# Normalising attention's output before a SwiGLU block: 32x32 transpositions on VectorE and one product in place of four sums and four transposes on TensorE

## The chip, the core and the metric

The kernel runs on one core of one Trainium2 chip. A time is the device time of one execution in microseconds (us). It stands here as the median of several runs; the profile is of one execution, in which every instruction on each engine has a start and a duration. [...] Each engine runs its own queue in order and waits on semaphores of the others.

## What is computed

Attention with normalised queries and keys, followed by a feed-forward block with a normalisation ahead of it (all f32, 8 sequences of 448 rows, 12 heads of 64, model width 768, inner width 1536):

```python
q_n, k_n = rmsnorm(q, g_q), rmsnorm(k, g_k)          # over the 64 of a head
scores = matmul(q_n, k_n.T) / sqrt(64)
attn = exp(scores - max); attn = attn / (sum(attn) + 1e-9)
x = (attn @ v) laid out as (8 * 448, 768)

rms = sqrt(mean(x * x, axis=-1) + 1e-6)
xn = x / rms * rms_g
g = xn @ w_gate
out = (g * sigmoid(g) * (xn @ w_val)) @ w_out
```

The change is in how `rms` of x is formed and spread.

## The kernel before

The kernel works on pairs of heads, six to a sequence, 48 in all, in one loop whose index is g = 6 b + hp. Attention's output for a pair comes out transposed: x of sequence b is a tile of 128 partitions (features of the pair) by 448 columns (rows of the sequence), six such tiles to a sequence. The sum of squares over the 768 features is therefore a sum over partitions and over the six tiles. ScalarE squares each pair's x, GpSimd adds it to the tile `ss` (128 x 448, L644), so that after the sixth pair each column of `ss` still has to be summed over 128 partitions.

Two functions finish it:

- `rms_x(b)` (L721 to L730): four products with a column of ones, one for each 112 columns of `ss`, which put the 448 sums into PSUM as 112 partitions x 4 columns (`msx`, L726); VectorE scales them and adds 1e-6 (L728), GpSimd raises to the power -0.5 (L730).
- `norm_x(b)` (L732 on): four transposes on TensorE of those columns, broadcast to 128 (L738), which give `rb`, the 448 factors on all partitions, in PSUM; six VectorE instructions multiply x by the gain and by `rb` (L744), spread over the next steps for b > 0. It then queues the sums of x blocks that the fast products read.

Sequence b of the feed-forward runs while attention of sequence b+1 goes on. Its products are done by a scheme with fewer multiplications, so that VectorE makes sums of blocks of x, of the weights and of the results (L1209, L1212, L1378, L1406 and others). Weight sums are made once, in sequences 1 to 3: `derive` (L1091, L1094), `derive_o` (L1126) and `derive_q` (L1154 to L1157) write them, SyncE stores them to DRAM (`kept`, `kept_o`, `kept_q`) and loads them back for the products. Before that, while sequence 0 is under way, the weights themselves are taken in and converted in three steps on VectorE (L917 to L919), two on ScalarE (L911, L912) and one on GpSimd (L968).

The order of all this is written out by hand. The main loop calls `pe(fn)` for each piece of TensorE work, `fill(n)` puts n pieces of feed-forward products between pieces of attention, and `after(n, fn)` has a piece of another engine's work issued n TensorE pieces later. No scheduler moves anything, so what is issued first on an engine runs first there. At the first pair of a sequence (hp == 0, b of 2 and more) the loop turns the next pair's queries and keys (`turn`, L545 and L549, transposes on TensorE), issues `rms_x(b - 1)` between the two turns, finishes the feed-forward products in hand (L1604 in sequence 0, L1191 after) with `fill(len(todo))`, and then issues `norm_x(b - 1)`. For sequence 0 the two functions are called one pair later, with their own lines. `invert` (L597 to L599) is in use for attention's sums: it transposes 32x32 blocks on VectorE, inverts 14 columns, and transposes them back with a broadcast.

PSUM holds four banks for scores (tag `s`, from which `msx` and `rb` are taken), one for attention's values and three for feed-forward products.

## Time and profile before

| | |
|---|---|
| three runs, us | 1515.65, 1513.07, 1515.41 |
| median, us | 1515.41 |
| span of the profiled execution, us | 1514.0 |
| granted TensorE clock, mean over the span | 0.997 |
| instructions in the span | 25709 |
| TensorE weight loads | 8732 |
| DMA | 322.51 MB, mean 213 GB/s |

The profiled execution is known by its span, from its first to its last instruction; the runs also hold what lies around that. The page gives each engine's busy time and the chain of work that ended last; further views give, for one line or tile, the durations of its instructions, for one engine what it waited for and what ended the wait, and for a stretch of time each instruction with its start. "PE" is TensorE's products, "PEld" its weight loads, "SPq" the issue of DMAs. A product of f32 tiles is recorded as two passes, a transpose as one.

### The profile page before, as it was taken

To read this page: it belongs to the slowest core of one execution; us is meant where nothing else is said; L and a number is where in the kernel's file an instruction comes from. 1 tells how busy PE (TensorE), PEld (TensorE's weight loads), DVE (VectorE), ACT (ScalarE), POOL (GpSimd) and SP (SyncE) were. 2 spreads that over 40 slices of the span, in tenths; PEclk is the share of its full clock that TensorE was granted. 3 is DMA by queue.
4 is the path that set the end of the run, shared out by engine and by line. 5 is a ranking of instruction groups with operands and counts; after the bars stand their busy time and mean duration, and the time that the engine had idled before them with its cause. 6 is when DMAs were issued, how large, how long until landed. Compare 5 with 4: busy or idle time off the path is not lost.

```text
span 1514.0 us, 25709 instructions
## 1 busy us (share of the span) xinstructions
PE 1478.8 (98%) x8732; PEld 1154.0 (76%) x8732; DVE 1037.7 (69%) x1826; ACT 602.2 (40%) x1377; POOL 741.3 (49%) x708
## 2 busy tenths in 40 slices
PE   8999999999899999999999999999999999999997
PEld 4344445678755888878888888768888789899997
DVE  5788999699944697874568555535668655684664
ACT  6856764344323433234343443443542433101100
POOL 6867997556423454564535643445645731021002
PEclk9999999999999999999999999999999999999999
DMA  7758675776667899996558855585558655587675
GB/s 200 227 159 252 174 247 174 228 249 206 224 219 224 266 316 312 301 291 180 163 150 257 244 176 153 165 255 159 153 153 255 216 162 139 165 292 234 174 228 180
DMA packets 302176, 322.51 MB, mean 213 GB/s; under 512 B 81620, under 2 KB 243668, under 8 KB 302036
## 3 DMA queue, kind: packets, MB, share of 16 engines
q1 hardware_dynamic: 301108, 320.58, 69.4%
q8 instruction: 72, 1.18, 0.3%
q14 instruction: 68, 0.56, 0.1%
q10 hardware_dynamic: 800, 0.20, 0.1%
q0 software_dynamic: 128, 0.00, 0.0%
HBM read 266.90 MB, written 53.77 MB: 212 GB/s over the span
## 4 chain that ended last, share of the span: by engine, by line
PE 84%; DVE 8%; DMA 3%; issue 1%; SPq 1%; POOL 1%; ACT 0%; DVEq 0%; POOLq 0%
PE ff L1191 37%; PE ff L1532 13%; PE sc L659 7%; PE av L674 7%; PE ff L1604 6%; PE ff L1461 5%; PE tr L545 2%; PE den L692 1%; PE den L607 1%; PE sc L563 1%; PE av L590 1%; PE ff L1334 1%; DVE l L1406 1%; DMA w<-kept 1%; DVE w L1091 1%
## 5 line engine op out<-in xcount | busy, mean ns | idle before, releaser
L1191 PE MATMUL ff<-x,w 128*128 128x224 f32 x1296 | 259.6, 353 | 1.4 <-DVE pb L1212 1.1
L714 POOL TENSOR_TENSOR es<-es,e 128x448 f32<-128x448 f32 x205 | 253.4, 1236 | 13.6
L1191 PEld LDWEIGHTS ff<-x,w 128*128 128x128 f32 x1296 | 242.7, 190 | 5.4 <-DVE pb L1212 1.4
L659 PE MATMUL sc<-qT,kT 64*64 64x448 f32 x1176 | 231.0, 539 | 0.7 <-DVE x L744 0.7
L674 PE MATMUL av<-e,vt 64*64 64x448 f32 x984 | 193.1, 538 | 0.0
L664 ACT ACTIVATE e<-sc 128x448 f32<-128x448 f32 x294 | 154.2, 547 | 72.6 <-PE sc L659 57.1
L1191 PE MATMUL ff<-xs,w 128*128 128x224 f32 x832 | 165.0, 353 | 2.9 <-issue 1.6
L1191 PEld LDWEIGHTS ff<-xs,w 128*128 128x128 f32 x832 | 155.7, 190 | 6.2 <-issue 3.0
L644 POOL TENSOR_TENSOR ss<-ss,rd 128x448 f32<-128x448 f32 x40 | 47.1, 1178 | 207.2 <-ACT rd L643 206.5
L709 POOL TENSOR_TENSOR es<-e 128x448 f32<-128x448 f32 x41 | 49.2, 1200 | 192.3 <-ACT e L664 192.3
L659 PEld LDWEIGHTS sc<-qT,kT 64*64 64x64 f32 x1176 | 79.2, 133 | 82.1 <-issue 60.1
L1532 PE MATMUL ff<-w,l 128*128 128x192 f32 x630 | 117.8, 328 | 3.7 <-DVE pa L1567 1.7
L515 POOL TENSOR_TENSOR rs<-ms,mhalf 128x12 f32<-128x12 f32 (+1 forms) x50 | 115.9, 2319 | 4.2
L1212 DVE TENSOR_TENSOR pc<-ff,l 128x448 f32<-128x448 f32 x56 | 34.8, 622 | 115.7 <-PE ff L1191 80.9
L1604 PE MATMUL ff<-x,w 128*128 128x448 f32 x288 | 111.8, 541 | 0.0
L1532 PEld LDWEIGHTS ff<-w,l 128*128 128x128 f32 x630 | 103.8, 190 | 8.7 <-DVE pa L1567 2.9
L674 PEld LDWEIGHTS av<-e,vt 64*64 64x64 f32 x984 | 66.0, 133 | 41.6 <-issue 41.6
L1604 PEld LDWEIGHTS ff<-x,w 128*128 128x128 f32 x288 | 53.3, 190 | 51.1 <-issue 48.2
L1191 PE MATMUL ff<-top_x,w 128*128 128x224 f32 x440 | 91.1, 356 | 0.0
L1209 DVE TENSOR_TENSOR pb<-ff,pb 128x448 f32<-128x448 f32 x84 | 52.3, 623 | 56.1 <-PE ff L1191 50.3
L1191 PEld LDWEIGHTS ff<-top_x,w 128*128 128x128 f32 x440 | 81.8, 190 | 11.3 <-issue 8.5
L1191 PE MATMUL ff<-l,w 128*128 128x224 f32 x416 | 83.6, 353 | 1.1 <-DVE pc L1212 1.1
(212 smaller groups left out, 2806.1 us busy)
## 6 DMA issues: line engine op xcount, KB each, us to landing
w<-kept SPq DMA_DIRECT2D x380, 256.0 KB, 3.5
w<-kept_q SPq DMA_DIRECT2D x350, 192.0 KB, 3.8
w<-kept_o SPq DMA_DIRECT2D x150, 192.0 KB, 3.6
kept_q<-w SPq DMA_DIRECT2D x63, 192.0 KB, 3.9
qk<-in_q_dram SPq DMA_DIRECT2D x48, 192.0 KB, 3.7
qk<-in_k_dram SPq DMA_DIRECT2D x96, 96.0 KB, 3.7
raw<-in_moe_w_gate_dram SPq DMA_DIRECT2D x24, 384.0 KB, 4.8
raw<-in_moe_w_val_dram SPq DMA_DIRECT2D x24, 384.0 KB, 4.4
```

What stands on the lines that cost most here:

```text
L515: nc.gpsimd.tensor_tensor(st["rs", g][:, cols], ms, mhalf[:, cols], ALU.pow)
L644: after(m, lambda: (nc.gpsimd.tensor_tensor(ss, ss, rd, ALU.add), st.update({("summed", b): hp})))
L659: nc.tensor.matmul(ps[r, 0:S], lhsT=st["kT", g][r, keys_of(i)], rhs=st["qT", g][r, :], start=True, stop=True)
L664: nc.scalar.activation(e, ps[:, 0:S], ACT.Exp)
L674: nc.tensor.matmul(st["av", g][own(j), 0:S], lhsT=vt, rhs=st["e", g, i][r], start=i == 0, stop=i == PARTS - 1, skip_group_check=True)
L709: nc.gpsimd.tensor_tensor(st["es", g], st["e", g, 0], st["e", g, 1], ALU.add)
L714: nc.gpsimd.tensor_tensor(st["es", g], st["es", g], st["e", g, i], ALU.add)
L1191: nc.tensor.matmul(bank[:, w * HT:(w + 1) * HT], lhsT=data(key)[:, (2 * w + c) * 128:(2 * w + c + 1) * 128], rhs=a[left][:, c, :], start=o ...
L1209: nc.vector.tensor_tensor(T[name], ps[:, 0:S], T[name], ALU.add)
L1461: nc.tensor.matmul(ps, lhsT=left_o(b, which, LEFT_O[name], c), rhs=data(("wo", b, name, c)), start=first and c == 0, stop=c == NFP - 1, sk ...
L1532: nc.tensor.matmul(ps, lhsT=a[:, j, :], rhs=data(key)[:, n % 2 * HW:(n % 2 + 1) * HW], start=start and j == 0, stop=j == KG - 1, skip_grou ...
L1604: nc.tensor.matmul(bank[w][:, 0:S], lhsT=data(key)[:, c * 128:(c + 1) * 128], rhs=st["x", 0][:, 3 * half + c, :], start=half == c == 0, st ...
```

## The change

For sequences 1 to 7 the sum over partitions is split. `fold_x`, new, lets VectorE transpose `ss` in place in blocks of 32x32, so that within each quarter of 32 partitions a column's parts lie along a row, and add each 32 of them into one: `few_x`, 128 x 14. One product with a constant 128x128 matrix `alike`, whose entry is 1 where the two indices are equal modulo 32, adds the four quarters and leaves the sums on all of them. VectorE scales (L738 after), GpSimd raises 128 x 14 numbers to the power, and in `norm_x` VectorE transposes them back with a broadcast into the tile of `ss`, in SBUF, from which the six scalings read. The order changes too: `fold_x` is issued ahead of the last `fill(1)`, and the product behind the second turn. Sequence 0 keeps its way. The constant is built by four VectorE instructions near the start of the run; to make room, the tile `row` is taken from the pool of output tiles, and `mhalf` (the exponents) has 14 columns.

```diff
@@ rms_qk
-        nc.gpsimd.tensor_tensor(st["rs", g][:, cols], ms, mhalf[:, cols], ALU.pow)
+        nc.gpsimd.tensor_tensor(st["rs", g][:, cols], ms, mhalf[:, 0:cols.stop - cols.start], ALU.pow)
@@
+    def blocks(t):
+        return t.rearrange("p (n c) -> p n c", c=32)
+
+    def fold_x(b):
+
+        assert st["summed", b] == NPAIR - 1
+        ss = st["ss", b]
+        nc.vector.transpose(out=blocks(ss), in_=blocks(ss))
+        few = st["few_x", b] = tmp.tile([128, S // 32], F32, name="few_x", tag="few_x", bufs=1)
+        nc.vector.tensor_reduce(out=few, in_=blocks(ss), axis=AX_X, op=ALU.add)
+
     def rms_x(b):
+        if b:
+            few = st.pop(("few_x", b))
+            ps = ps_s.tile([128, 512], F32, name="msx", tag="s")
+            nc.tensor.matmul(ps[:, 0:S // 32], lhsT=alike, rhs=few, start=True, stop=True)
+            ms = st["rx", b] = tmp.tile([128, S // 32], F32, name="rx", tag="rx", bufs=1)
+            nc.vector.tensor_scalar(ms, ps[:, 0:S // 32], 1.0 / DM, 1e-6, ALU.mult, ALU.add)
+            nc.gpsimd.tensor_tensor(ms, ms, mhalf, ALU.pow)
+            return
@@ norm_x
-        ps = (ps_s if b else ps_f).tile([128, 512], F32, name="rb", tag="s" if b else "f")
-        for t in range(NT):
-            nc.tensor.transpose(ps[:, t * P:(t + 1) * P], rs[:, t:t + 1].to_broadcast([P, 128]), ident[0:P, 0:P])
+        if b:
+            ps = st.pop(("ss", b))
+            nc.vector.transpose(out=blocks(ps), in_=rs.unsqueeze(2).to_broadcast([128, S // 32, 32]))
+        else:
...
@@
-    mhalf = const.tile([128, 4 * NK], F32, name="mhalf")
+    mhalf = const.tile([128, S // 32], F32, name="mhalf")
@@
-    row = const.tile([1, 2, D], F32, name="row")
+    row = y_pool.tile([1, 2, D], F32, name="y", tag="y")
+    alike = const.tile([128, 128], F32, name="alike")
+
+    def one_per_quarter():
+
+        nc.vector.tensor_reduce(out=alike[:, 0:32], in_=ident.rearrange("p (n c) -> p c n", c=32), axis=AX_X, op=ALU.add)
+        for n in range(1, 4):
+            nc.vector.tensor_copy(alike[:, n * 32:(n + 1) * 32], alike[:, 0:32])
@@ the main loop, g == 2
                 bound()
+                one_per_quarter()
@@ the main loop, first pair of a sequence
         norm_k(g + 1, 1)
+        if b > 1:
+            fold_x(b - 1)
         fill(1)
-        pe(lambda: rms_x(b - 1))
+        if b == 1:
+            pe(lambda: rms_x(b - 1))
         squares(g + 2, 0)
         squares(g + 2, 1)
         pe(lambda: turn(g + 1, 1))
+        if b > 1:
+            pe(lambda: rms_x(b - 1))
         fill(len(todo))
         begin(b - 1, 16)
         pe(lambda: norm_x(b - 1))
```

How the order of instructions changes can be seen on two engines, at three places. Line numbers of the changed kernel are higher by 23 or so. First TensorE in sequence 1, where the sums and the spreading of its x stand among the last products of sequence 0's feed-forward (`ff`) and the turns of queries and keys (`tr`); before:

```order
L549 MATMUL tr<-ident,rest 128x128
L1604 MATMUL ff<-x,w 128x448 x3
L726 MATMUL msx<-ones,ss 112x1 x4
L545 MATMUL tr<-ident,qk 128x128 x3
L1604 MATMUL ff<-x,w 128x448 x12
L738 MATMUL rb<-ident,rs_2403 128x112 x4
L1334 MATMUL ff<-w,h_123 128x384 x3
```

and after:

```order
L549 MATMUL tr<-ident,rest 128x128
L1627 MATMUL ff<-x,w 128x448 x3
L545 MATMUL tr<-ident,qk 128x128 x3
L736 MATMUL msx<-few_x,alike 128x14
L1627 MATMUL ff<-x,w 128x448 x12
L1357 MATMUL ff<-w,h_123 128x384 x3
```

The four sums and the four transposes are gone, and the one product stands three transposes later, ahead of the same twelve products.

Next VectorE at the same place, among conversions of weights (`top`, `top_x`) and the feed-forward's element work (`h`); before:

```order
L1613 SCALAR_TENSOR_TENSOR h_126<-th,ff 128x448
L917 TENSOR_SCALAR top<-top 128x384
L918 TENSOR_SCALAR top<-top 128x384
L919 SCALAR_TENSOR_TENSOR top<-raw,top 128x384
L1615 SCALAR_TENSOR_TENSOR h_126<-h_126,ff 128x448
L917 TENSOR_SCALAR top_x<-top_x 128x384
L918 TENSOR_SCALAR top_x<-top_x 128x384
L919 SCALAR_TENSOR_TENSOR top_x<-raw,top_x 128x384
L728 TENSOR_SCALAR ms_2401<-msx 112x4
L496 TENSOR_REDUCE ms<-sq 128x6 x2
```

and after:

```order
L1636 SCALAR_TENSOR_TENSOR h_126<-th,ff 128x448
L940 TENSOR_SCALAR top<-top 128x384
L941 TENSOR_SCALAR top<-top 128x384
L942 SCALAR_TENSOR_TENSOR top<-raw,top 128x384
L728 STREAM_TRANSPOSE ss<-ss 128x448
L730 TENSOR_REDUCE few_x<-ss 128x14
L1638 SCALAR_TENSOR_TENSOR h_126<-h_126,ff 128x448
L940 TENSOR_SCALAR top_x<-top_x 128x384
L941 TENSOR_SCALAR top_x<-top_x 128x384
L942 SCALAR_TENSOR_TENSOR top_x<-raw,top_x 128x384
L496 TENSOR_REDUCE ms<-sq 128x6 x2
L738 TENSOR_SCALAR rx<-msx 128x14
```

The fold's two instructions stand behind one more set of conversions and ahead of the feed-forward's second product with `h`; the scaling of the sums moves behind the two reductions.

Last VectorE in sequence 5, where no weights are converted or summed; before:

```order
L1212 TENSOR_TENSOR pc<-ff,l_7745 128x448
L1209 TENSOR_TENSOR pb<-ff,pb 128x448
L1209 TENSOR_TENSOR pa<-ff,pa 128x448
L728 TENSOR_SCALAR ms_8614<-msx 112x4
L496 TENSOR_REDUCE ms<-sq 128x6 x2
L1209 TENSOR_TENSOR pa<-ff,pa 128x448
```

and after:

```order
L1235 TENSOR_TENSOR pc<-ff,l_7730 128x448
L1232 TENSOR_TENSOR pb<-ff,pb 128x448
L728 STREAM_TRANSPOSE ss<-ss 128x448
L730 TENSOR_REDUCE few_x<-ss 128x14
L1232 TENSOR_TENSOR pa<-ff,pa 128x448
L496 TENSOR_REDUCE ms<-sq 128x6 x2
L738 TENSOR_SCALAR rx<-msx 128x14
L1232 TENSOR_TENSOR pa<-ff,pa 128x448
```

Here the fold stands directly behind the `pb` that ends the instructions of the product before, and ahead of the `pa` of the next.

## The prediction

> **What bounds the kernel now.** I read the page first, for which engine has no slack, then the waits of TensorE, then the timeline around each place where a sequence's x is normalised. On the page the first line gives busy time by engine, the second the chain that ended last.

> ```profile
> PE 1478.8 (98%) x8732; PEld 1154.0 (76%) x8732; DVE 1037.7 (69%) x1826; ACT 602.2 (40%) x1377; POOL 741.3 (49%) x708
> PE 84%; DVE 8%; DMA 3%; issue 1%; SPq 1%; POOL 1%; ACT 0%; DVEq 0%; POOLq 0%
> ```

> TensorE is busy 98% of the span and holds 84% of the chain. What it does less is gained, and what it waits more is lost, unless a wait behind it swallows the difference. VectorE at 69% looks free, but that is a mean, and the question here is how far VectorE is behind TensorE at seven moments. The longest waits that TensorE has now, in the view of waits (total us, times, longest), show where a delay could be swallowed:

> ```profile
> PE ff L1461 <- DMA w<-kept_o: 3.6, 1, 3.6
> PE ff L1191 <- DVE pb L1209: 3.2, 2, 2.4
> ```

> They are few and short. I call the sequences 0 to 7; the change works on 1 to 7, so each step below comes seven times.

> **What the change removes.** In sequence 1 TensorE's timeline (start, us, engine, line) reads:

> ```profile
> 228.15 0.85 PE L726 MATMUL msx<-ones,ss 128*112 128x1 f32 x8
> 228.87 0.53 PE L545 MATMUL tr<-ident,qk 128*128 128x128 f32 x3
> 229.23 9.19 PE L1604 MATMUL ff<-x,w 128*128 128x448 f32 x24
> 238.25 0.55 PE L738 MATMUL rb<-ident,rs 112*128 112x112 f32 x4
> 238.64 7.92 PE L1334 MATMUL ff<-w,h 128*128 128x384 f32 x24
> ```

> Starts tell what TensorE gives up, since matmuls overlap. The four sums are eight records (an f32 product runs as two passes) and hold the engine from 228.15 to 228.87: 0.72 us. The four spreading transposes take it from 238.25 to 238.64: 0.39. The one new product is again two passes, with a stationary tile of 128 columns. The nearest rows put a pass between 0.09 (0.72 / 8) and 0.12 (three transpositions of 128x128 from 228.87 to 229.23), so 0.18 to 0.24; I take 0.22, near the upper row, whose weights are also 128 wide. Without any wait TensorE thus saves 0.72 + 0.39 - 0.22 = 0.89 us a sequence, 6.2 in all.

> **What it adds on VectorE.** First the prices: ns least/median/most for the first four, then two timeline rows.

> ```profile
> L597 DVE STREAM_TRANSPOSE rd<-rd x41: 631/639/649, 115.4 to 1296.3; 128x448 f32<-128x448 f32 x41
> L496 DVE TENSOR_REDUCE ms<-sq x96: 530/543/554, 4.1 to 1217.5; 128x6 f32<-128x384 f32 x96
> L515 POOL TENSOR_TENSOR rs<-ms,mhalf x50: 1350/2300/2901, 5.1 to 1218.4; 128x12 f32<-128x12 f32 x46, 128x6 f32<-128x6 f32 x4
> L744 DVE SCALAR_TENSOR_TENSOR x<-x,rg,rb x48: 668/675/681, 91.9 to 1326.2; 128x448 f32<-128x448 f32 x48
> 412.02 0.62 DVE L1223 SCALAR_TENSOR_TENSOR h<-th,pa 128x448 f32<-128x448 f32 x1
> 394.51 1.50 DVE L1264 TENSOR_TENSOR pc<-pc,l 128x448 f32<-128x448 f32 x1
> ```

> The fold is a transposition, 0.64, and a sum over 448 elements. The sum over 384 takes 0.54, so this one takes 0.54 to 0.63 (by length), and I take the longer: 1.3 us with the step between them, and 0.06 more until TensorE sees it (the pb row and the TensorE row of sequence 2 below are that far apart). The second transposition adds 0.64 where the scaled x is made. The scalings get their third operand from SBUF: between 0.62 (L1223) and 1.50 (L1264, also two operands in SBUF) in place of 0.675, so from -2.3 to +35 us over 42. I take the lower end: the chance of a long one is left to the range. They hang on no product within the next few microseconds, and VectorE has 476 us idle; were that cover gone, the upper end would be paid. The root on GpSimd grows from 4 to 14 columns, about 2.3 to 2.9 by the L515 row; several VectorE rows stand between it and the second transposition in every order, which hide it. Four small instructions building the constant near 35 us, and the row buffer that moves, lie beside an attention stage in which TensorE waits for nothing like them: 0, or at most about 1 us if they stood on the path (two of L496's price).

> **The new wait.** The sums of before read ss, which GpSimd finishes early. The new product reads what VectorE folds, and VectorE's queue is in order. So at each place I set two times beside each other: when VectorE comes to the fold (the start of the instruction that follows it now) and when TensorE comes to the product (its next start now, less the 0.72 removed). In sequence 1:

> ```profile
> 222.66 1.25 POOL L644 TENSOR_TENSOR ss<-ss,rd 128x448 f32<-128x448 f32 x1
> 231.13 0.61 DVE L1613 SCALAR_TENSOR_TENSOR h<-th,ff 128x448 f32<-128x448 f32 x1
> 233.53 0.56 DVE L919 SCALAR_TENSOR_TENSOR top<-raw,top 128x384 int32<-128x384 int32 x1
> 234.00 0.61 DVE L1615 SCALAR_TENSOR_TENSOR h<-h,ff 128x448 f32<-128x448 f32 x1
> 249.67 0.59 PE L659 MATMUL sc<-qT,kT 64*64 64x448 f32 x2 [0.69 <-DVE x L744]
> ```

> ss is complete at 223.9, but VectorE is deep in weight conversion. By the order, the fold stands between L919 and L1615, so it starts at 234.0 and TensorE can go on at 235.36. TensorE is there at 229.23 - 0.72 = 228.51. It waits 6.85 us, and behind the product are queued 24 passes of L1604 that need nothing of it. One wait goes: the score bank held by rb until the scaling, 0.69, because rb is no longer in PSUM. Sequence 1: 6.85 - 0.89 - 0.69 = +5.3. Behind it the next long wait is far and VectorE then waits for TensorE, so I let nothing absorb it.

> In sequence 2 the path is different. The rows are TensorE, VectorE and SyncE's queue:

> ```profile
> 402.73 1.68 PE L1191 MATMUL ff<-x,raw 128*128 128x224 f32 x8
> 405.19 0.62 DVE L1209 TENSOR_TENSOR pa<-ff,pa 128x448 f32<-128x448 f32 x1
> 409.36 0.62 DVE L1209 TENSOR_TENSOR pb<-ff,pb 128x448 f32<-128x448 f32 x1
> 410.04 1.78 PE L1191 MATMUL ff<-raw,w 128*128 128x224 f32 x8 [2.39 <-DVE pb L1209]
> 414.69 2.18 SPq L1070 DMA_DIRECT2D w<-kept_o  x4
> 418.43 2.19 PE L1461 MATMUL ff<-w,top 128*128 128x384 f32 x4 [3.63 <-DMA w<-kept_o]
> ```

> TensorE arrives at 402.73 - 0.72 = 402.01, the fold starts at 405.19 and is done at 406.55: a wait of 4.5. But TensorE now loses 2.39 and 3.63 behind it anyway, to VectorE's pb and to a load that itself follows weight sums VectorE makes. Those come 1.3 later, by the fold, and TensorE, which reaches the first of these waits 4.5 - 0.72 + 0.22 = 4.0 late, has that much taken up. Between -0.9 (all absorbed) and +3.6 (nothing): I take the 1.3 of VectorE's chain.

> In sequence 3 it is alike, with shorter waits behind:

> ```profile
> 600.35 4.71 PE L1191 MATMUL ff<-x,w 128*128 128x224 f32 x24
> 601.95 0.62 DVE L1209 TENSOR_TENSOR pa<-ff,pa 128x448 f32<-128x448 f32 x1
> 605.88 1.78 PE L1191 MATMUL ff<-raw,w 128*128 128x224 f32 x8 [0.82 <-DVE pb L1209]
> 608.18 0.61 DVE L1209 TENSOR_TENSOR pc<-ff,pc 128x448 f32<-128x448 f32 x1
> 615.16 2.19 PE L1532 MATMUL ff<-w,top 128*128 128x192 f32 x12 [1.25 <-DMA w<-kept_q]
> ```

> The fold is done at 601.95 + 1.36 = 603.31 and TensorE arrives at 599.63: 3.7 of wait, so the 24 passes start 3.2 late. The 0.82 takes some of it, which leaves 2.3; the pc that reads the next product is then 2.3 late, and so are the sums and the load behind it. I take +2.3, between -0.9 and +2.8.

> From sequence 4 on VectorE has no weight sums left and is close behind TensorE:

> ```profile
> 782.42 0.89 DVE L1406 TENSOR_TENSOR h<-h 128x384 f32<-128x384 f32 x1
> 783.63 0.85 PE L726 MATMUL msx<-ones,ss 128*112 128x1 f32 x8
> 963.66 0.62 DVE L1209 TENSOR_TENSOR pb<-ff,pb 128x448 f32<-128x448 f32 x1 [0.89 <-PE ff L1191]
> 965.41 0.85 PE L726 MATMUL msx<-ones,ss 128*112 128x1 f32 x8
> 1306.52 0.55 DVE L1406 TENSOR_TENSOR h<-top,h 128x384 f32<-128x384 f32 x1
> 1307.29 0.86 PE L726 MATMUL msx<-ones,ss 128*112 128x1 f32 x8
> ```

> Sequence 4: the fold goes from 783.31 to 784.67, TensorE arrives after three transposes (0.36) at 783.99, so 0.7 - 0.9 = -0.2. Sequence 5: folded by 965.64, arrival 965.77, so the full -0.9. Sequence 6 has sequence 4's order, and I take its -0.2. Sequence 7 has no transposes between: folded by 1308.43, arrival 1307.29, so 1.1 - 0.9 = +0.2. Together -1.1.

> **The clock.** TensorE's idle time can cost once more. After the 3.63 us at 418.43 the windows show (columns: length, TensorE, weight loads, VectorE, ScalarE, GpSimd, granted clock, DMA share, GB/s):

> ```profile
> 419.30:422.60 3.30, 3.30 (x7) 1.79 (x6) 3.20 (x7) 0.48 (x1) 0.00 (x0) 0.50 1.04 364
> ```

> At half clock for 3.3 us the engine does 1.7 us less. The wait of 6.85 is longer than the one that caused it, so it should set off one such stretch, part of which may fall into the wait itself: 0 to 1.7, and I take 1.2. For the shorter waits of sequences 2 and 3, I take none, because the chains through VectorE and the loads set their end. [...]

> **The sum.** 5.3 + 1.3 + 2.3 - 1.1 + 1.2 = +9.0. On the profiled span of 1514.0 that is 1523.0. The median of the three runs shown, 1515.41, lies 1.4 above that span, so I forecast 1524.4.

> **The rivals.** *The gain arrives*: if VectorE reached the folds in time, only the 6.2 would be left: 1509.2. It is the case of the other side; it decides wherever the fold starts at least 1.36 us ahead of TensorE's arrival, or as soon as all seven waits add up to under 6.2. For it speaks sequence 5; against it 234.00, 405.19 and 601.95, all well after the arrivals. 0.10.

> *The waits are given back*: sequences 2 and 3 lose nothing by them (their 2.39, 3.63, 0.82 and 1.25 absorb everything), and no half clock follows. Then 5.3 - 1.1 = +4.2: 1519.6. For it: a load may not hang on the late VectorE rows. Against it: those loads follow sums that VectorE makes behind the fold. 0.15.

> *Three cold stretches*: each of the 6.85, 4.5 and 3.7 us idles is longer than the 3.63 that brought the 0.50 row. If each halves the clock for a whole stretch and the path takes it, 3 x 1.7 stands in place of 1.2: +3.9, so 1528.3. For it: the one case in the trace. Against it: the waits behind sequences 2 and 3 may hide it, and one case fixes no threshold. 0.17.

> **The numbers.** The forecast keeps 0.58. About 0.2% (3 us) is what a measurement of this kernel can tell from no change. The range goes from 1516.5, below the second rival by the part of sequence 1's wait that I may have overcounted (3 us), to 1530.0, above the third by some long scalings. Faster by over 0.2%: 0.10, the first rival. Within: 0.05, the low edge of the second. Slower: 0.85.

> **What would show it.** Right: a wait of TensorE for VectorE's few_x, about 6.8, 4.5 and 3.7 us in sequences 1 to 3 and under 1.2 after; a granted clock of 0.50 soon after the first; L659's 0.69 gone; the kept_o and kept_q loads landing 1 to 2.5 later relative to the product. Wrong: the product in sequence 1 starting with less than 3 us of wait, or VectorE's rows there standing earlier than now. The forecast falls if those three waits add up to less than 6, or if later waits of TensorE shrink by as much as these bring.

## The result and the profile after

The changed kernel takes 1525.45 us (median of five runs, 1524.62 to 1526.55), beside 1515.41 for the kernel before (five runs, 1513.07 to 1518.69): a ratio of 1.0066, 95% interval 1.0048 to 1.0084. The forecast was 1524.4. The total is close, but two of its terms were wrong by about 4 and 5 us, in opposite directions, as the traces show.

The page of the changed kernel, busy time by engine (DVE is VectorE, ACT ScalarE, POOL GpSimd, SP SyncE) and the chain that ended last:

```profile
PE 1480.7 (97%) x8662; PEld 1154.7 (76%) x8662; DVE 1062.7 (70%) x1851; ACT 601.5 (39%) x1377; POOL 753.0 (49%) x708
PE 85%; DVE 10%; issue 1%; SPq 1%; DMA 1%; ACT 0%; POOL 0%; DVEq 0%
```

TensorE has 70 records fewer and yet is busy 1.9 us longer: some of its work ran at a lower clock, 0.50 in the windows further down. Of the chain that ended last, VectorE's part grew from 8 to 10%, and the DMAs' fell from 3 to 1%. TensorE's waits (total, times, longest) have a new first row:

```profile
PE msx L736 <- DVE few_x L730: 16.3, 6, 6.7
PE ff L1555 <- DVE pa L1590: 2.7, 4, 1.2
...
PE ff L1555 <- DMA w<-kept_q: 0.5, 1, 0.5
```

Before's two longest waits, for kept_o (3.6) and for pb (3.2), are not in this list. The new operations by line (ns least/median/most):

```profile
L728 DVE STREAM_TRANSPOSE ss<-ss x7: 632/636/639, 236.2 to 1315.9; 128x448 f32<-128x448 f32 x7
L730 DVE TENSOR_REDUCE few_x<-ss x7: 619/620/620, 236.8 to 1316.5; 128x14 f32<-128x448 f32 x7
L739 POOL TENSOR_TENSOR rx<-rx,mhalf x7: 2595/2597/2640, 240.3 to 1317.9; 128x14 f32<-128x14 f32 x7
L767 DVE SCALAR_TENSOR_TENSOR x<-x,rg,ss x42: 671/677/1557, 253.0 to 1336.2; 128x448 f32<-128x448 f32 x42
```

The fold costs 0.64 + 0.62. Most scalings from SBUF cost what those from PSUM did (677 beside 675), but the longest took 1557. Two of the 42 took over 0.7 us (1132 and 1557 ns), and both overlap a GpSimd instruction. The timeline of sequences 1 to 3, TensorE at the new product (start, us, with the idle time before it in brackets):

```profile
237.52 0.61 PE L736 MATMUL msx<-few_x,alike 128*128 128x14 f32 x2 [6.70 <-DVE few_x L730]
...
416.21 0.61 PE L736 MATMUL msx<-few_x,alike 128*128 128x14 f32 x2 [4.35 <-DVE few_x L730]
...
609.15 0.61 PE L736 MATMUL msx<-few_x,alike 128*128 128x14 f32 x2 [3.50 <-DVE few_x L730]
```

And the windows around them (TensorE's busy time is the first number after the length, the granted clock the third from the end):

```profile
229.71:233.12 3.41, 1.11 (x6) 0.45 (x4) 3.34 (x3) 2.98 (x8) 3.33 (x4) 1.00 0.66 178
233.12:236.53 3.41, 0.00 (x0) 0.00 (x0) 3.34 (x6) 0.00 (x0) 2.37 (x3) 0.50 0.58 152
236.53:239.95 3.42, 2.43 (x5) 1.60 (x6) 3.32 (x8) 0.00 (x0) 0.96 (x1) 0.50 0.88 193
239.95:243.36 3.41, 3.41 (x6) 1.38 (x5) 2.68 (x8) 0.00 (x0) 2.88 (x2) 0.50 0.40 150
243.36:246.77 3.41, 3.41 (x11) 1.74 (x10) 0.76 (x2) 1.34 (x4) 3.31 (x4) 1.00 0.01 2
410.61:414.03 3.42, 1.25 (x8) 0.96 (x6) 3.39 (x4) 2.06 (x8) 3.17 (x3) 1.00 0.00 0
414.03:420.86 6.83, 4.65 (x13) 4.29 (x14) 5.45 (x12) 0.17 (x1) 2.03 (x1) 0.50 0.70 247
605.17:608.59 3.42, 0.49 (x4) 0.25 (x2) 3.35 (x6) 1.30 (x4) 1.76 (x2) 1.00 0.64 212
608.59:612.00 3.41, 2.85 (x9) 2.63 (x10) 2.04 (x5) 0.00 (x0) 1.29 (x1) 0.50 0.98 299
612.00:615.41 3.41, 3.41 (x11) 3.08 (x10) 1.80 (x5) 0.58 (x1) 3.24 (x3) 0.50 0.21 69
```

Between 20 and 1500 us there are three stretches at half clock. TensorE worked 2.43 + 3.41 = 5.84 us of the first at half speed, 4.65 of the second and 6.26 of the third, which costs about half of each: 2.9, 2.3 and 3.1 us. Before had one, of 3.4.

To place the 10 us I set the same score products of two profiles beside each other and took how far each came later than in before's profile. The columns give the growth of that lag up to the score products of sequence 1 ("start"), across the normalisation of sequence 1, 2, between 2 and 3, across 3, 4, 5 and 6, from ahead of 7 to the last product, and over the whole span to the start of TensorE's last product:

```
                    start seq1  seq2  2-3   seq3  seq4  seq5  seq6  seq7  all
after               +2.2  +7.5  -2.5  -1.3  +4.3  -0.2  -0.9  -0.2  +1.1  +10.0
e2_warm_wait        +0.5  +4.7  -3.0  -0.0  +1.5  -0.2  -0.9  -0.2  +1.1   +3.5
e3_only_from_4      +0.5  +0.0  -1.2  -1.0  -0.5  -0.2  -0.9  -0.2  +1.1   -2.4
e4_fold_unread      +2.4  +2.3  -1.5  -0.6  +0.2   0.0   0.0   0.0  +0.5   +3.4
e1_late_product     +0.4  +4.2  -1.7  -1.2  -0.7  -0.9  -0.9  -0.9  -0.5   -0.9
e5_spread_psum      +2.0  +5.6  -1.7  -0.6  -0.7  -0.9  -0.9  -0.9  -0.5   +3.3
e6_late_from_4      +0.1  +0.1  -0.1  +0.1  -0.2  -0.9  -0.9  -0.9  -0.5   -3.1
e8_early_fold       +2.0  +3.5  -0.8  -1.6  +0.4  -0.9  -0.9  -0.9   0.0   +0.8
e7_before_again     +1.9   0.0  -0.1  -1.5  -0.1   0.0   0.0   0.0   0.0   +0.2
e9_early_and_two    +0.6  +4.6  -2.3  -1.0   0.0  -0.9  -0.9  -0.9   0.0   -0.8
e10_old_in_1        +1.7  +0.7  -2.0  -1.0  +0.1  -0.9  -0.9  -0.9   0.0   -3.2
```

What is missing from a row's sum lies between the columns (0.1, but 1.4 and 1.9 in e1 and e5). The row e7 is the unchanged kernel a second time: +1.9 at the start and -1.5 between sequences 2 and 3 are what two profiles of one kernel differ by, though over the whole span they differ by 0.2. The row e3 leaves sequences 1 to 3 as they were, and its -1.2, -1.0 and -0.5 from sequence 2 to sequence 3 are chance too. The columns of sequences 1 and 4 to 7 are 0.0 in e7, and that of sequence 1 is 0.0 and +0.1 in e3 and e6, which leave it alone; the readings below rest on these columns. A row is one execution: that of e9 was the fastest of its twelve runs (1515.01 beside a median of 1517.36) and that of e3 the third fastest (1513.28 beside 1515.62), so a row's last column and the medians below need not agree.

### The profile page after: what moved, and what is told of

Same layout as the page of the kernel before. It is cut to its first block, busy times and chain, and to the rows that moved or that the text cites. A ratio compares the mean times of both kernels' runs of the same rounds, so it can differ in the third digit from the quotient of the medians.

```text
span 1523.7 us, 25572 instructions
## 1 busy us (share of the span) xinstructions
PE 1480.7 (97%) x8662; PEld 1154.7 (76%) x8662; DVE 1062.7 (70%) x1851; ACT 601.5 (39%) x1377; POOL 753.0 (49%) x708
## 4 chain that ended last, share of the span: by engine, by line
PE 85%; DVE 10%; issue 1%; SPq 1%; DMA 1%; ACT 0%; POOL 0%; DVEq 0%
PE ff L1214 38%; PE ff L1555 13%; PE sc L659 8%; PE av L674 7%; PE ff L1627 6%; PE ff L1484 5%; PE ff L1357 2%; PE tr L545 1%; PE den L692 1%; DVE l L1429 1%; PE den L607 1%; PE sc L563 1%; PE av L590 1%; DVE top L942 1%; DVE w L1114 0%
## 5 line engine op out<-in xcount | busy, mean ns | idle before, releaser
L1214 PE MATMUL ff<-x,w 128*128 128x224 f32 x1296 | 263.1, 357 | 1.4 <-DVE pb L1235 1.1
L1214 PEld LDWEIGHTS ff<-x,w 128*128 128x128 f32 x1296 | 245.8, 192 | 5.6 <-DVE pb L1235 1.4
L659 PE MATMUL sc<-qT,kT 64*64 64x448 f32 x1176 | 230.8, 539 | 0.0
L644 POOL TENSOR_TENSOR ss<-ss,rd 128x448 f32<-128x448 f32 x40 | 47.3, 1182 | 205.1 <-ACT rd L643 204.5
L659 PEld LDWEIGHTS sc<-qT,kT 64*64 64x64 f32 x1176 | 79.2, 133 | 81.2 <-issue 61.6
L515 POOL TENSOR_TENSOR rs<-ms,mhalf 128x12 f32<-128x12 f32 (+1 forms) x50 | 115.0, 2299 | 4.2
L1627 PEld LDWEIGHTS ff<-x,w 128*128 128x128 f32 x288 | 54.5, 194 | 52.6 <-issue 49.7
L1526 POOL TENSOR_TENSOR y<-y,pa 128x384 f32<-128x384 f32 x10 | 11.4, 1154 | 149.5 <-DMA w<-kept_q 112.1
```

The source lines that it names most:

```text
L515: nc.gpsimd.tensor_tensor(st["rs", g][:, cols], ms, mhalf[:, 0:cols.stop - cols.start], ALU.pow)
L644: after(m, lambda: (nc.gpsimd.tensor_tensor(ss, ss, rd, ALU.add), st.update({("summed", b): hp})))
L659: nc.tensor.matmul(ps[r, 0:S], lhsT=st["kT", g][r, keys_of(i)], rhs=st["qT", g][r, :], start=True, stop=True)
L1214: nc.tensor.matmul(bank[:, w * HT:(w + 1) * HT], lhsT=data(key)[:, (2 * w + c) * 128:(2 * w + c + 1) * 128], rhs=a[left][:, c, :], start=o ...
L1627: nc.tensor.matmul(bank[w][:, 0:S], lhsT=data(key)[:, c * 128:(c + 1) * 128], rhs=st["x", 0][:, 3 * half + c, :], start=half == c == 0, st ...
```

## The experiments

Two theories stood at first. One: the loss is the waits for few_x and the half clock behind them, and an order that lets few_x come in time brings the gain. The other: VectorE's added work itself is the loss in sequence 1, wherever TensorE waits for it. Diffs are against the changed kernel, and "..." or the words beside a diff stand for what it leaves out.

**The clock alone (e2).** TensorE does unread products in front of the three long waits (they fill PSUM columns that nobody reads), so it isn't idle there.

```diff
+            for _ in range({1: 27, 2: 17, 3: 14}.get(b, 0)):
+                nc.tensor.matmul(ps[:, 128:256], lhsT=ident, rhs=ident, start=True, stop=True)
```

> The changed kernel with 27, 17 and 14 products of 128x128, read by nobody, in front of the new product in sequences 1, 2 and 3, about as long as TensorE waits there. They change nothing of when few_x is there, only that TensorE runs meanwhile. If the half clock behind the waits is a part of the loss (2.9, 2.3 and 3.1 us of it fall behind the waits in the trace, some of it hidden): clock 1.0 behind all three, 1517 to 1521. If it is hidden or has no share: 1524 to 1527. [...]

Measured 1519.48 (before 1515.55; ratio 1.0036, 1.0022 to 1.005). The windows of the changed kernel around the three places, then its own:

```profile
220.00:280.00 60.00, 53.30 (x198) 28.44 (x197) 51.17 (x73) 26.21 (x63) 45.19 (x39) 0.91 0.55 171
380.00:440.00 60.00, 55.65 (x325) 43.19 (x324) 55.03 (x87) 22.40 (x50) 25.52 (x21) 0.94 0.75 241
580.00:640.00 60.00, 55.93 (x351) 46.49 (x350) 50.62 (x97) 19.47 (x43) 21.39 (x17) 0.94 0.89 284
```

```profile
220.00:280.00 60.00, 59.29 (x281) 34.48 (x283) 48.04 (x72) 26.41 (x64) 43.04 (x38) 1.00 0.59 180
380.00:440.00 60.00, 58.23 (x350) 43.38 (x349) 47.85 (x80) 20.89 (x46) 26.84 (x22) 1.00 0.70 227
580.00:640.00 60.00, 58.00 (x394) 49.37 (x395) 52.33 (x99) 21.13 (x51) 25.97 (x21) 1.00 0.94 297
```

The clock is 1.00 in all three, in place of 0.91, 0.94 and 0.94. VectorE's order and the time at which few_x comes are as in the changed kernel. So the half clock costs 1525.45 - 1519.48 = 6.0 us; by the columns it is 2.8 in each of sequences 1 and 3 and 0.5 in 2. A wait filled with unread work is still a wait, but one without this second price.

**Only the sequences from 4 on (e3).** Sequences 1 to 3 are normalised the old way.

```diff
-        if b:
+        if b > 3:
...
```

> Sequences 4 to 7 have the new way, 1 to 3 the old. Theory: the waits there are 0.4, 0, 0.4 and 0.9 us against 0.89 saved in each, so 1.9 us gained at the most: 1513 to 1516. Rival (each sequence's added VectorE work costs about the same): four sevenths of the loss of 10, so about 1521.

Measured 1515.62 (ratio 1.0005, 0.9994 to 1.0016). The rival falls: sequences 4 to 7 bring -0.2, -0.9, -0.2 and +1.1, within 0.02 as in the changed kernel, so that the new operations take nothing there in sum. But for 0.5 at the start (the constant, below), the loss lies in sequences 1 to 3.

**The added VectorE work, read by nobody (e4).** The old sums and spreads stay, and VectorE folds a spare tile one of TensorE's pieces later than in the changed kernel, and transposes it at the changed kernel's place. What is left out is any use of the fold.

```diff
+        pe(lambda: rms_x(b - 1))
+        fold_x(b - 1)
...
+            nc.vector.transpose(out=blocks(st["spare_x"]), in_=st["few_x", b].unsqueeze(2).to_broadcast([128, S // 32, 32]))
```

> TensorE's four sums and four transposes stay as before, and VectorE's transposition, sum and second transposition are added one piece later, with nobody reading them. It prices VectorE's added work without the wait. Theory: 1515 to 1519, the upper end if VectorE's chain in sequences 2 and 3 comes 1.3 us later each. Rival (the added work on VectorE is the loss): 1522 to 1526.

Measured 1519.0 (ratio 1.0027, 1.0015 to 1.0039), at the upper end of what was expected. One of TensorE's waits:

```profile
PE sc L659 <- DVE x L764: 3.0, 1, 3.0
```

In sequence 1 the score bank is released 3.0 late where before it was 0.69, and that difference is the whole +2.3 of that column: 1.9 us of VectorE's time ahead of the scalings go onto the path without any product that reads them. The columns of sequences 4 to 6 are 0.0: there the same work is free.

**The product later (e1).** The product stands behind the other pieces that follow it in the block, and the second transposition and the scalings two of TensorE's pieces later.

```diff
+    LATE = 2
...
+        fill(len(todo) - 1)
+        pe(lambda: rms_x(b - 1))
...
```

> The product stands behind all but the last piece of the feed-forward products in hand, and the spreading and the scalings two TensorE pieces later; all of the change's work stays. Theory (TensorE waits for few_x in sequences 1 to 3, behind VectorE's backlog): the waits of 6.7, 4.4 and 3.5 us shrink to under 1 us in all, no half clock follows, and the 6.2 us of TensorE work come through: 1507 to 1512, against 1515.4 before. Rival (VectorE's added work, or the scalings that read SBUF, set the time): the work is all there, so 1522 or more.

Measured 1516.08 (ratio 1.001, 1.0001 to 1.0019): outside the first theory's 1507 to 1512, and its rival's 1522 or more. There is no wait for few_x any more, and sequences 3 to 7 gain 3.9 (1.4 of which is lost again between 3 and 4), but sequence 1 still loses 4.2. Its waits, and VectorE's timeline there:

```profile
PE ff L1359 <- POOL w L993: 1.9, 1, 1.9
PE sc L659 <- ACT e L664: 1.9, 1, 1.9
```

```profile
248.53 0.65 DVE L759 STREAM_TRANSPOSE ss<-rx 128x448 f32<-128x448 f32 x1 [0.62 <-POOL rx L741]
249.21 3.46 DVE L769 SCALAR_TENSOR_TENSOR x<-x,rg,ss 128x448 f32<-128x448 f32 x3
...
253.88 2.63 DVE L769 SCALAR_TENSOR_TENSOR x<-x,rg,ss 128x448 f32<-128x448 f32 x3
```

The six scalings, three at a time, took 3.46 and 2.63 us (1.15 and 0.88 each; three took 1.85 before, 0.62 each). They stand ahead of the weight conversion, which goes from VectorE to GpSimd and ends in the tile w that TensorE waits for. Of the 4.2, 1.9 + 1.9 - 0.89 - 0.69 = 2.2 are waits less savings, and a stretch at half clock adds up to 1.7:

```profile
248.51:251.92 3.41, 1.52 (x20) 0.46 (x16) 3.35 (x4) 2.22 (x6) 3.41 (x3) 1.00 0.88 233
251.92:255.33 3.41, 3.41 (x25) 1.52 (x18) 3.31 (x6) 3.12 (x8) 1.40 (x2) 1.00 0.99 338
268.99:272.40 3.41, 1.53 (x4) 0.79 (x5) 0.44 (x1) 0.00 (x0) 3.41 (x4) 1.00 0.17 60
272.40:275.81 3.41, 3.41 (x6) 1.69 (x5) 0.00 (x0) 0.48 (x1) 1.54 (x2) 0.50 0.90 274
```

So both theories had a part of it, and neither was enough.

**The spread into PSUM (e5).** As the run before, but the second transposition writes a PSUM bank, so that a scaling has only one large operand in SBUF again.

```diff
+            ps = ps_s.tile([128, 512], F32, name="rb", tag="s")
+            after(LATE, lambda: nc.vector.transpose(out=blocks(ps[:, 0:S]), in_=rs.unsqueeze(2).to_broadcast([128, S // 32, 32])))
```

> The late product (1516.1) with one edit: the second transposition writes a PSUM bank, so the six scalings read PSUM as before the change. With the late product sequence 1 still loses 4.2 us though TensorE no longer waits for few_x; its six scalings take 6.1 us there in place of 3.6. Theory 2 (behind the wait, VectorE's conversion backlog bounds sequence 1, and scalings with two SBUF operands beside GpSimd lengthen it): scalings back at about 0.68 us, sequence 1's loss 1.5 to 2.5, total 1513 to 1515. Rival (the fold and GpSimd's longer root alone make it): 4.2 stays, 1516.

Measured 1519.6 (before 1514.77; ratio 1.0028, 1.0016 to 1.004): slower than both theories allowed, because the edit brought a wait of its own. Two rows of its timeline in sequence 1:

```profile
250.84 1.86 DVE L770 SCALAR_TENSOR_TENSOR x<-x,rg,rb 128x448 f32<-128x448 f32 x3
...
256.09 1.01 PE L659 MATMUL sc<-qT,kT 64*64 64x448 f32 x2 [5.85 <-DVE x L770]
```

Three scalings are back at 1.86 (0.62 each), in place of the late product's 3.46, with GpSimd as busy beside them: 3.41 us of the window from 249.18 on here, 3.41 of that from 248.51 on there. But the bank is one of the score products', and they wait 5.85 us until the late scalings are through. As a test of the total the run is inconclusive; what it shows is the scalings' price.

**The later product, from sequence 4 on (e6).** Sequences 1 to 3 the old way, the rest as in the late product, and the constant built at sequence 4.

```diff
-        if b > 1:
+        if b > 4:
+            fill(len(todo) - 1)
             pe(lambda: rms_x(b - 1))
...
+        if g == 27:
+            one_per_quarter()
...
```

> The old way in sequences 1 to 3, the new way with the late product in 4 to 7, and the constant built in sequence 4. Theory: 0.89 us gained in each of sequences 4 to 6 and about 0.5 in 7, 0.5 not lost at the start: 1511.5 to 1513.0 against 1515.5 before. Rival (the saved TensorE work comes back as waits for VectorE further on): 1515 to 1516.

Measured 1512.28 (1510.63 to 1513.46; before 1514.77; ratio 0.998, 0.997 to 0.999): faster than both kernels. Three columns hold -0.9 and the last -0.5, together -3.2 of the -3.1 in all. One of TensorE's waits:

```profile
PE ff L1555 <- DVE pa L1590: 1.5, 3, 0.5
```

In the changed kernel this row reads 2.7, 4, 1.2: with the transposition out of the way the last sequence gains as well.

**The fold earlier (e8).** The fold two of TensorE's pieces earlier, the product where the change has it.

```diff
-        fill(2)
+        fill(1)
+        if b > 1:
+            fold_x(b - 1)
+        fill(1)
         pe(lambda: turn(g + 1, 0))
         norm_k(g + 1, 1)
-        if b > 1:
-            fold_x(b - 1)
```

> The changed kernel with the fold issued two TensorE pieces earlier, the product where the change has it. By VectorE's rows the waits come down to about 3.9, 2.4 and 0 us in sequences 1 to 3, and to 0 after. If the wait alone sets sequence 1's loss, that is 1.8 us plus a half clock of at most 1.7: 1512 to 1514. If VectorE's backlog is a floor under it (theory 2), 4.2 stays: 1514.5 to 1517.

Measured 1516.68 (ratio 1.0012, 1.0003 to 1.0021). The waits for few_x are 3.84 and 2.36 in sequences 1 and 2 and none in 3 and later (both in one row):

```profile
PE msx L736 <- DVE few_x L730: 6.2, 2, 3.8
```

Sequence 1 lost 3.5: 3.84 - 0.89 - 0.69 = 2.3, and one half-clock window of 3.4 us (1.7), less 0.5 that no view names. So nothing held it at the late product's 4.2; the total, though, is where that floor would have put it. For this comparison the unchanged kernel was profiled a second time.

> The kernel before once more, for a second profile of it. If the differences outside the seven places (2.2 us at the start, 1.3 between sequences 2 and 3, a shorter wait for kept_o) are chance, this profile will show such differences from the first one too: spans 1510 to 1517.

It gave 1515.69; its row in the table is, with e3's, the measure of chance used above.

**Early fold and later product (e9).** As with the early fold, and with the product behind two more feed-forward pieces in sequences 1 and 2, so that nobody waits for few_x there.

```diff
+        fill(2 if b < 4 else 0)
         if b > 1:
             pe(lambda: rms_x(b - 1))
```

> VectorE's product and sum stand two pieces of TensorE's work earlier in every sequence, and in sequences 1 and 2 the product with few_x stands behind two more feed-forward pieces, so that nothing waits for few_x in sequences 1 to 3; the scalings stand where the change has them. Theory (the waits for few_x and the half clock behind them are the whole loss): no wait for few_x, no half clock after sequences 1 and 3, sequence 1 between -1.6 and +0.5, the later sequences -0.9 each; total 1509 to 1512 beside 1514 to 1515.5 for the kernel before. Rival (in sequence 1 VectorE's backlog is the floor: the scalings come late beside GpSimd's work and something else of theirs is waited for, 2.3 to 4.2 us as in the runs with the unread fold and the late product): sequence 1 again above +2, and a total of 1513 to 1516.

Measured 1517.36 (before 1515.09; ratio 1.0017, 1.0008 to 1.0027). The waits for few_x are gone, and sequence 1 loses 4.6: the rival's condition, though the total lies above its range too. The trace, like its row in the table, is of one run of 1515.01 and shows nothing of what the others lost beyond it. TensorE's waits, then VectorE's, GpSimd's and ScalarE's timelines:

```profile
PE ff L1357 <- POOL w L991: 3.2, 1, 3.2
...
PE sc L659 <- ACT e L664: 1.5, 1, 1.5
```

```profile
247.38 0.65 DVE L757 STREAM_TRANSPOSE ss<-rx 128x448 f32<-128x448 f32 x1 [1.49 <-POOL rx L739]
248.06 5.24 DVE L767 SCALAR_TENSOR_TENSOR x<-x,rg,ss 128x448 f32<-128x448 f32 x6
```

```profile
244.65 2.70 POOL L739 TENSOR_TENSOR rx<-rx,mhalf 128x14 f32<-128x14 f32 x1
247.32 3.72 POOL L991 TENSOR_TENSOR w<-top,raw 128x384 int32<-128x384 int32 x3
...
249.38 0.55 ACT L934 ACTIVATE top<-raw 128x384 f32<-128x384 f32 x1 [0.88 <-DMA raw<-in_moe_w_out_dram]
```

Here the chain can be read: few_x comes in time, but the root of 14 columns takes 2.70 on GpSimd, VectorE is idle 1.49 waiting for it, the six scalings then take 5.24 beside GpSimd's conversions, and the conversions behind them reach TensorE 3.2 late. The 1.5 for e comes by way of ScalarE, whose conversion waits 0.88 for a load of `raw` (issued at 248.36, after the first of GpSimd's three conversions behind the root) and stands ahead of the exponentials e. 3.2 + 1.5 - 0.89 - 0.69 is 3.1, and a half-clock window from 271.7 on adds up to 1.7. How much of this the longer root alone makes is not shown: e4 keeps it short, but its scalings also read PSUM.

**The same with sequence 1 the old way (e10).**

```diff
-        if b:
+        if b > 1:
...
+        if g == 13:
+            one_per_quarter()
...
```

> As the run before it, but sequence 1 is normalized the old way and the constant for the new way is built after sequence 1. Theory (sequence 1 has no room on VectorE and GpSimd, the later sequences have): sequence 1 at 0, no wait for few_x in the rest, sequences 3 to 6 at -0.9 each or a little less, total 1510 to 1512.5. Rival (sequences 2 and 3 lose something else, as with the late product, where two waits of 1.9 us came): 1514 to 1516.

Measured 1513.05 (1510.35 to 1513.8; ratio 0.9986, 0.9977 to 0.9995): faster than before, a little above the theory's range. Sequences 4 to 6 have the full -0.9, sequence 3 gains nothing, and of sequence 2's -2.0 chance alone can make 1.2, as in e3. Sequence 1 loses 0.7, though TensorE's order in it is the old one. VectorE builds the constant there, among the conversions, and TensorE then waits for a converted w as it doesn't in before:

```profile
256.93 2.07 DVE L1777 COPY alike<-alike 128x32 f32<-128x32 f32 x3
...
270.30 4.47 PE L1357 MATMUL ff<-w,h 128*128 128x384 f32 x12 [0.41 <-POOL w L991]
```

Of the 0.7 the lag grows by 0.6 between the score products ahead of the constant and the next ones behind it, and e3, which normalises sequence 1 in the same way and order and has the constant elsewhere, loses 0.0. By its total the kernel can't be told apart from the version from sequence 4 on. So the new way pays where VectorE and GpSimd convert no weights, shows no loss beyond chance in 2 and 3 if fold and product stand as here, and loses in 1 in each of the five orders tried (the change's, late, PSUM, early, early with a later product: +7.5, +4.2, +5.6, +3.5, +4.6).

## Why the prediction was right, and where it was wrong

*TensorE's saving of 0.89 a sequence*: right. Sequence 5 measured -0.90, and three sequences of each later kernel -0.89.

*The prices*: right for the fold (0.64 + 0.62) and the root (2.60). The scalings from SBUF cost nothing at the median; some reach 1557 ns, which was left to the range. That they "hang on no product within the next few microseconds" held only while the wait for few_x covered them: in e9 their 5.24 us stand ahead of conversions that TensorE waits for.

*The waits* of 6.85, 4.5, 3.7, 0.7, 0, 0.7 and 1.1: measured 6.70, 4.35, 3.50, 0.42, 0, 0.41 and 0.88. Reading VectorE's queue from the old trace and TensorE's arrival beside it gave every one to 0.3.

*Sequence 1, +5.3 and no clock*: +4.7 with the clock kept up. Right to 0.6. That this is mainly a wait for few_x was right for the kernel as changed, but incomplete: with that wait gone (e1, e9) others stand there, the longest 1.9 and 3.2.

*The clock, 1.2*: wrong, and the largest error. The step that failed is "For the shorter waits of sequences 2 and 3, I take none", along with one stretch of 3.3 for the first. There were three, 10.2, 6.8 and 6.8 long, and they cost 6.0. The rival of three cold stretches had the mechanism and a low price (1.7 each; 2.8 were measured in sequences 1 and 3).

*Sequence 2, +1.3*: wrong. The step that failed: kept_o's load "follows weight sums VectorE makes", so that it would come 1.3 later and the wait of 3.63 stay. Two timeline rows of the changed kernel:

```profile
424.11 1.89 SPq L1093 DMA_DIRECT2D w<-kept_o  x4
...
424.86 4.03 PE L1484 MATMUL ff<-w,top 128*128 128x384 f32 x12
```

The load is issued 424.11 - 414.69 = 9.4 after before's, while the sequence as a whole began 9.7 late; it did not slip at all. TensorE comes to its third piece about 12.7 late (427.5, after eight of these twelve products, in place of 418.43 - 3.63 = 414.80) and finds the load landed. The wait for few_x is therefore paid by waits that go: 4.35 - 0.89 - 2.39 - 3.63 = -2.6, and 0.6 more half clock than before (2.3 in place of 1.7), so -2.0; -2.5 was measured. Chance has a part in this column: in e3, where sequence 2 is unchanged, the wait for kept_o is 2.4 in place of 3.6 and the column holds -1.2. It can't make up the 3.8 between +1.3 and -2.5. This part of the rival in which the waits are given back was right.

*Sequence 3, +2.3*: 3.50 - 0.89 - 0.82 - 0.7 (the kept_q wait fell from 1.25 to 0.55) = +1.1 before the clock, +1.5 with the clock kept up, +4.3 with the 3.1 of half clock. The mechanism was right, the size 0.8 too large: the forecast's "3.2 late" leaves in the 0.4 of the four spreading transposes, and it let the wait for kept_q stand, which fell by 0.7.

*Sequences 4 to 6*: -0.2, -0.9 and -0.2 were forecast and measured.

*Sequence 7, +0.2*: +1.1. The term that was missing is the second transposition, for which I had counted no time on the path. TensorE in before's timeline, then VectorE and TensorE in the changed kernel's:

```profile
1322.72 2.22 PE L1532 MATMUL ff<-w,l 128*128 128x192 f32 x12 [0.22 <-DVE pa L1567]
```

```profile
1322.28 1.16 DVE L1232 TENSOR_TENSOR pc<-ff,pc 128x448 f32<-128x448 f32 x2 [0.89 <-PE ff L1214]
...
1325.08 0.64 DVE L757 STREAM_TRANSPOSE ss<-rx 128x448 f32<-128x448 f32 x1
...
1332.11 0.55 DVE L1590 TENSOR_TENSOR pa<-ff,th 128x384 f32<-128x384 f32 x1
...
1332.71 2.22 PE L1555 MATMUL ff<-w,l 128*128 128x192 f32 x12 [1.16 <-DVE pa L1590]
```

VectorE runs without a pause from 1322.28 to this pa; the transposition pushes it back by 0.55 (it starts 9.83 behind the pc, in before 9.28: 1312.83 and 1322.11). TensorE, which no longer does the four spreading transposes, comes there 0.39 earlier, so that its wait of 0.22 became 1.16. In e4, which keeps these transposes, the wait is 0.74. An earlier fold leaves that as it is (0.0 in all, with the fold's own wait gone); the version from sequence 4 on, which scales two of TensorE's pieces later, has no wait above 0.5 for this pa (its row above).

*The constant, 0*: too low by 0.5. In each of the eight kernels that build it near 45 us the lag grows by 0.53 to 0.55 between the score products at 49 and 59 us; in e6 and e10, which build it later, and in e7 it grows by 0.0. The rest of the start column, -0.2 to +1.9, is there at the first score product, at 11 us, ahead of the constant, and the unchanged kernel has +1.8 of it: chance.

So the sign and the main place were right. That the total came so close was luck: the clock was 4.8 too low, and sequence 2, with the clock kept up -3.0 beside the forecast's +1.3, was 4.3 too high.

## What to carry to other kernels

Moving work from a saturated engine to one with idle time on average is worth only what the receiving engine's queue leaves at that moment: place the added instructions in each stage's trace, and take the change only in the stages where that queue is near empty, as the version from sequence 4 on does. When one wait is taken away, look for the next one behind it before counting the gain; here sequence 1 had a second chain, through the conversions, which kept 4.2 and 4.6 of its 7.5 us lost. An idle stretch on TensorE can have a second price, here 6.0 us of half clock after three of them, which can be read by filling the stretches with unread products.
